# TensorE weights 128 columns wide in place of 125 in a fused Branchformer forward and backward kernel

## The chip, the cores and the metric

The kernel runs on one core of one Trainium2 chip, in one launch. The metric is device time in microseconds. Three runs of the kernel before gave 1264.24, 1264.71 and 1265.43 us, median 1264.71.

Names used below: PE is the matrix engine (TensorE), PEld its weight loads, DVE the vector engine, ACT the scalar engine, POOL the GpSimd engine, SP the engine that issues most DMAs. A product on PE has two operands: the *weights*, which are loaded into the array first by an instruction of their own, and the *moving* operand, whose columns are then streamed through. The number of weight columns is the number of output partitions; the number of moving columns is the free size of the output.

## The reference

One Branchformer layer, forward and gradient of all inputs, for x of shape 2 x 4000 x 144 in bf16. Cut to what matters:

```python
xa = _layernorm(x)
q, k, v = split(xa @ w_qkv)
p = softmax(q @ k.T * D ** -0.5)              # 4000 x 4000 for each of 2 batches
glob = (p @ v) @ w_att_out
u, g = split(gelu(_layernorm(x) @ w_mlp_in))
gc = sum(pad(_layernorm(g))[i:i+T] * dw_csgu[i] for i in range(5))
loc = (u * gc) @ w_mlp_out
m = concat(glob, loc); m = m + depthwise_conv5(m, dw_merge)
out = x + m @ w_merge
# returned: out and the vector-Jacobian products of grad_out for x and the seven weights
```

## The kernel before

The 4000 tokens of a batch are split into NB = 32 tiles of PB = 125 tokens. So nearly every weight operand that holds a tile of tokens is 125 columns wide. The four large buffers that hold such tiles already keep them 128 apart: P and dP scores in `Pb` and `SX`, their transposes PT and ST in `SX`. The three columns between are zeroed once by `pads` (line 953) for the score buffers, and the transposes on the DMA rings read and write all 128.

`phase_att` runs once per batch. It loops over t, the tile of queries. In each turn:

- `quad` (lines 1024 and 1030) makes score chunks of 125 x 500: for two chunks of scores (q of tile t) and two of dP (tile t-1) it issues four products with 128 rows of weights `QT` (line 1024, 500 moving columns), and then the four remaining products with 16 rows each (line 1030), whose weights stand in four different groups of 32 rows of the array and so can run side by side. I call the eight a quad.
- DVE takes the score chunks out of PSUM with a running minimum (line 1048), ACT takes the exponential (1056), ACT and DVE make P times dP (1066, 1069, 1071).
- The DMA rings transpose P into PT (1060) and P times dP into ST (1251).
- `Y_half` (1080) and `Z_half` (1126) run 32 products each over PT and ST with 145 and 144 moving columns. `X_group` (1171) runs products with the untransposed score buffers as weights and 144 moving columns, with a few more from `zt` and `dhT`; DVE adds them to the accumulator (1177).
- The units of the local branch (`local_units`) are dealt out over the turns. `t_unit` (595) transposes the gate and its gradient, with weights already 128 columns wide (`gdr`), into the tiles `gT` (line 502, five blocks of 125 columns). `gc_unit` (606, 607) and `dgn_unit` (621, 622) run the short convolution as ten products each, weights from `gT`, with 64 or 68 moving columns in eight of them and 32 or 34 in two. `dhT_unit` transposes `dhr` on the DMA ring.
- `jit_mm` (983, 984, 987), `z_unit` (526, 527) and `dug_unit` (558, 561) take weights straight from `R`, `xaT_m` and `goT`, where the tiles lie 125 apart.

After each batch, `Merge` computes the merged branch (1454, weights of 128 columns, is its largest part; 1551 and 1553 follow). The order of the instructions on every engine is written out by hand: `ORDER` lists it as differences of instruction numbers, and `Planner.plan` chains the instructions of an engine in that order. PE, DVE, ACT and POOL each run their list in order.

Of the kernel before, what the change touches and what calls it, by code (L numbers as in the profile page):

```python
# [15 lines left out]
D = 144  # L16
DR = 16
PB = 125
# [461 lines left out]
def local_units(k, W, b, S, A, es, DHT, ps_w):  # L480
# [21 lines left out]
    gT = [[pl.tile([128, 5, PB], BF, name="gT%d%d" % (a, i)) for i in range(2 + a)] for a in range(2)]  # L502
# [12 lines left out]
    for t_ in dhr:  # L515
        nc.gpsimd.memset(t_[:], 0.0)

# [72 lines left out]
    def t_unit(m):  # L590
        for a in range(2):
            pt = ps_w.tile([128, 5, 128], BF, tag="w")
            for j in range(5):
                x = 448 if j == 4 else 128 * j
                nc.tensor.transpose(pt[:, j, 0:PB], gv[:, a, place(m), x:x + 128], W.ident[0:PB, 0:PB])
            nc.scalar.copy(gT[a][m % (2 + a)][:], pt[:, :, 0:PB])
# [4 lines left out]
    def gc_unit(g):  # L601
        pc = ps_w.tile([PB, G2, D], F32, tag="w")
# [5 lines left out]
        nc.scalar.copy(gc[:], pc[:])  # L608
# [7 lines left out]
    def dgn_unit(g):  # L616
        pd = ps_w.tile([PB, G2, 9, 17], F32, tag="w")
        for n_, (m, x) in enumerate(wins(g)):
            t = gT[1][m % 3]
            for j in range(4):  # L620
                nc.tensor.matmul(pd[:, :, 2 * j:2 * j + 2, :].rearrange("p a b c -> p a (b c)"), t[:, j, :], W.eb[:, 8 * j + x:8 * j + x + 2, :], start=(n_ == 0 and j == 0), stop=(n_ == 1), skip_group_check=True)
            nc.tensor.matmul(pd[:, :, 8, :], t[:, 4, :], W.ebr[:, x:x + 2, :], start=False, stop=(n_ == 1), skip_group_check=True)
        rs, t = rsr[slot(g)], gd(g + 1, 0)
# [21 lines left out]
    def dhT_unit(g):  # L645
        dhT = sm.tile([128, 3 * G2, 128], BF, tag="dhT", bufs=3)
        nc.sync.dma_start_transpose(out=dhT[:], in_=dhr[g % 2][:].rearrange("p a b -> p (a b)"))
        for bi in range(G2):
            DHT[G2 * g + bi] = [dhT[:, 3 * bi + ct, 0:PB] for ct in range(3)]
# [71 lines left out]
for _s in """  # L721
PE 10 1 1 1 1 1 1 1 1 1 1 1 1 1 1 1 1 1 1 1 1 1 1 1 1 1 1 1 1 1 1 180 -179 182 -181 1 1 1 1 1 1 1 1 1 1 1 1 1 1 1 1 168 2 11 -180 1 1 1 1 1 1 1 1 1 1
# [33 lines left out]
DVE 9 127 -128 165 -14 31 1 5 -3 -1 5 -2 14 -15 18 -14 1 12 37 4 -51 -1 54 -52 1 47 -43 3 76 -81 44 -43 41 4 -21 -22 28 -23 19 6 -4 -19 78 -1 -76 1 1  # L756
# [47 lines left out]
Activation 148 1 -4 -1 2 78 -77 74 1 3 -74 80 4 -6 -79 77 13 1 22 89 5 -88 1 4 -32 30 83 -77 78 -6 8 -7 -49 6 1 4 4 37 -5 -20 6 4 -28 33 9 17 1 2 2 2  # L804
# [28 lines left out]
Pool 420 -260 24 251 -247 -2 -10 -39 50 -25 -23 293 -271 -21 294 2 -298 3 33 247 -244 27 -29 -33 95 -4 -48 -42 37 39 -37 100 -99 250 -157 4 -101 82  # L833
# [18 lines left out]
SP 0 172 -171 2 -1 151 -146 -3 1 149 -148 149 13 -16 19 -14 109 1 -101 3 -4 140 1 -136 -14 2 5 1 184 -16 1 -166 180 75 75 1 1 1 53 49 -47 -5 -45 5 13  # L852
# [17 lines left out]
class Planner:  # L870
# [24 lines left out]
    def plan(self, i0, i1):  # L895
# [23 lines left out]
        assert len(groups) == sum(len(v) for v in ORDER.values())  # L919
        order = ORDER  # L920
        for e in E:
            assert sorted(order[e]) == [x for x, g in enumerate(groups) if g["e"] == e]
        self.groups, self.order = groups, order
        for e in E:
            prev = None
            for g in order[e]:
# [6 lines left out]
def phase_att(k, W, b, S, A, M, head=None, late=None, extra=None):  # L933
# [6 lines left out]
    with ExitStack() as es:  # L940
# [24 lines left out]
        qbr = [qz[0:PB, QW * i:QW * i + 768].rearrange("p (a b) -> p a b", b=384)[:, :, 0:D] for i in range(3)]  # L965
        qrr = [qz[0:PB, QW * i + 128:QW * i + 384] for i in range(3)]
        znr = [qz[:, 3 * QW + 256 * i:3 * QW + 256 * (i + 1)] for i in range(2)]
# [33 lines left out]
        def jit_tr(i):  # L1001
            PL.tag("jt")
            qb = QB[i]
# [6 lines left out]
            for q, src in enumerate((qb[:, 0, 0:128], qrr[i % 3][:, 0:128], qrr[i % 3][:, 128:256], qb[:, 1, 0:128])):  # L1010
                nc.tensor.transpose(pt[:, q, 0:PB], src, W.ident[0:PB, 0:PB])
            qt = gw.tile([128, 4, 128], BF, tag="qt")
            nc.scalar.copy(qt[:, :, 0:PB], pt[:, :, 0:PB])
# [59 lines left out]
        def Y_half(i, h):  # L1073
            PL.tag("y%d" % h)
            if h == 0 and i not in YZ:
                yz = ps_yz.tile([PB, 2, 145], F32, tag="yz")
                YZ[i] = yz
# [969 lines left out]
```

## Time and profile before

| | |
|---|---|
| time, three runs | 1264.24 to 1265.43 us, median 1264.71 |
| profiled execution | span 1259.7 us from the first to the last instruction; no other time is listed for it, so the 5.0 us up to the median of the runs is taken as what lies around the span |
| granted TensorE clock, mean | 0.996 |
| PE busy | 1227.3 us, 15,890 products and as many weight loads |
| DVE, ACT, POOL busy | 1056.2, 740.4, 442.4 us |
| share of the chain that ended last | PE 74%, DVE 11%, DMA 9% |

How to read it: a row of instruction groups gives line, engine, operation, tile and shapes (partitions x columns; for PE the first pair is rows by columns of the weights), count, then busy time and mean duration. Durations of PE records overlap, since products are pipelined; the pace of products is seen in the chain view instead, whose rows are start, length and what ran, back to back. "issue" is time in which the engine waited for nothing that the profile shows.

### The profile page before, as it was taken

To read this page: it belongs to the slowest core of one execution; us is meant where nothing else is said; L and a number is where in the kernel's file an instruction comes from. 1 tells how busy PE (TensorE), PEld (TensorE's weight loads), DVE (VectorE), ACT (ScalarE), POOL (GpSimd) and SP (SyncE) were. 2 spreads that over 40 slices of the span, in tenths; PEclk is the share of its full clock that TensorE was granted. 3 is DMA by queue.
4 is the path that set the end of the run, shared out by engine and by line. 5 is a ranking of instruction groups with operands and counts; after the bars stand their busy time and mean duration, and the time that the engine had idled before them with its cause. 6 is when DMAs were issued, how large, how long until landed. Compare 5 with 4: busy or idle time off the path is not lost.

```text
span 1259.7 us, 38749 instructions
## 1 busy us (share of the span) xinstructions
PE 1227.3 (97%) x15890; PEld 1012.1 (80%) x15890; DVE 1056.2 (84%) x2862; ACT 740.4 (59%) x1183; POOL 442.4 (35%) x910
## 2 busy tenths in 40 slices
PE   9999999999999999999999999999999999999997
PEld 7777888878777878889887778788788888878996
DVE  8688989898988888879769898989888989887665
ACT  5866565556565655544746656565656565555273
POOL 8434333433333423213534423333334333232020
PEclk9999999999999999999999999999999999999998
DMA  3689988899989999985149989998898999999332
GB/s 106 129 146 151 158 157 157 156 151 154 168 146 157 158 151 159 158 193 159 65 101 157 161 158 164 155 160 146 145 173 151 155 157 162 172 167 188 96 103 69
DMA packets 638399, 186.52 MB, mean 148 GB/s; under 512 B 621025, under 2 KB 633164, under 8 KB 638214
## 3 DMA queue, kind: packets, MB, share of 16 engines
q1 hardware_dynamic: 616664, 176.66, 78.7%
q10 hardware_dynamic: 21348, 7.13, 3.0%
q8 instruction: 124, 2.03, 0.7%
q14 instruction: 55, 0.45, 0.1%
q0 software_dynamic: 208, 0.25, 0.1%
HBM read 20.82 MB, written 14.22 MB: 28 GB/s over the span
## 4 chain that ended last, share of the span: by engine, by line
PE 74%; DVE 11%; DMA 9%; ACT 2%; issue 2%; SPq 1%; POOL 1%; ACTq 0%; DVEq 0%
PE X L1171 17%; PE ps L1024 14%; PE yz L1126 9%; PE yz L1080 7%; PE ps L1030 6%; DMA SX<-SX 4%; PE Hps L1454 3%; PE po L1551 3%; DVE Pb L1048 3%; DMA SX<-Pb 2%; DVE acc L1177 1%; DMA qt<-qz 1%; PE pd L561 1%; PE pj L987 1%; PE pc L606 1%
## 5 line engine op out<-in xcount | busy, mean ns | idle before, releaser
L1048 DVE TENSOR_SCALAR_CACHE_REDUCE Pb<-ps 125x1000 bf16<-125x1000 f32 x256 | 306.2, 1197 | 75.8 <-PE ps L1030 71.5
L1056 ACT ACTIVATE Pb<-Pb,nm 125x1000 bf16<-125x1000 bf16 x256 | 277.4, 1127 | 120.5 <-DVE nm L1050 119.8
L1171 PE MATMUL X<-SX 125*125 125x144 bf16 x2048 | 300.1, 230 | 0.8 <-DVE acc L1175 0.7
L1171 PE MATMUL X<-SX,Pb 125*125 125x144 bf16 x2048 | 293.8, 226 | 0.0
L1069 ACT CAST SX<-ps 125x1000 bf16<-125x1000 f32 x189 | 187.9, 994 | 169.7 <-PE ps L1030 169.4
L1171 PEld LDWEIGHTS <-SX 125*125 125x125 bf16 x2048 | 259.8, 137 | 28.6 <-issue 28.0
L1024 PE MATMUL ps<-xaT_m,qt 128*125 128x500 bf16 x1024 | 262.2, 376 | 5.1 <-DVE Pb L1048 3.4
L1171 PEld LDWEIGHTS <-Pb 125*125 125x125 bf16 x2048 | 260.9, 137 | 1.4 <-issue 1.3
L1177 DVE TENSOR_TENSOR acc<-X,acc 125x432 f32<-125x432 f32 x372 | 200.9, 549 | 32.4 <-PE X L1171 31.2
L1126 PE MATMUL yz<-xa_aug,SX 125*125 125x144 bf16 x2048 | 153.0, 229 | 6.6 <-DMA SX<-SX 5.6
L1024 PEld LDWEIGHTS <-qt 128*125 128x125 bf16 x1024 | 122.1, 137 | 45.4 <-issue 5.0
L1126 PEld LDWEIGHTS <-SX 125*125 125x125 bf16 x2048 | 139.7, 138 | 14.0 <-DMA SX<-SX 7.8
L1080 PE MATMUL yz<-xa_aug,SX 125*125 125x145 bf16 x2048 | 145.9, 227 | 1.8 <-DMA SX<-Pb 1.8
L1080 PEld LDWEIGHTS <-SX 125*125 125x125 bf16 x2048 | 137.0, 137 | 3.2 <-DMA SX<-Pb 2.4
L1071 DVE TENSOR_TENSOR SX<-SX,Pb 125x1024 bf16<-125x1024 bf16 x189 | 130.8, 696 | 7.1 <-ACT SX L1069 4.8
L1030 PEld LDWEIGHTS <-qt 16*125 16x125 bf16 x1024 | 36.6, 128 | 99.7 <-issue 99.7
L1030 PE MATMUL ps<-XR,qt 16*125 16x500 bf16 x1016 | 112.1, 421 | 0.0
L1066 DVE TENSOR_TENSOR SX<-ps,Pb 125x1000 bf16<-125x1000 f32 x67 | 80.0, 1194 | 1.6 <-PE ps L1030 1.0
L635 POOL TENSOR_SCALAR l_w<-gdr,nc,c 125x144 f32<-125x144 bf16 x64 | 30.5, 480 | 97.1 <-DVE c L633 87.2
L531 POOL TENSOR_SCALAR l_a<-l_sq 125x576 bf16<-125x576 bf16 x32 | 23.1, 720 | 112.6 <-ACT l_sq L529 108.1
L1104 POOL TENSOR_SCALAR SX<-qz,rl 125x144 bf16<-125x144 bf16 x62 | 24.9, 402 | 96.9 <-DVE rl L1086 86.1
L999 POOL COPY qz<-qz 125x64 bf16<-125x64 bf16 (+1 forms) x124 | 33.4, 287 | 70.8 <-ACT qz L989 64.9
(474 smaller groups left out, 2179.4 us busy)
## 6 DMA issues: line engine op xcount, KB each, us to landing
go_h<-in_grad_out_dram SPq DMA_DIRECT2D x4, 567.0 KB
Yg<-ug_d SPq DMA_DIRECT2D x4, 567.0 KB
Yn_d<-yn ACTq DMA_DIRECT2D x64, 35.2 KB
Zn_d<-qz ACTq DMA_DIRECT2D x64, 35.2 KB
ug_d<-ugr ACTq DMA_DIRECT2D x32, 70.3 KB
SX<-in_x_dram SPq DMA_DIRECT2D x16, 140.6 KB
out_dram<-Pb SPq DMA_DIRECT2D x16, 140.6 KB
out_dram<-SX SPq DMA_DIRECT2D x16, 140.6 KB
```

What stands on the lines that cost most here:

```text
L1024: mm = nc.tensor.matmul(pp[r // 2][:, r % 2, 0:CH], QT[i][:, 3 * h, 0:PB], xaTm[:, c * CH:(c + 1) * CH], start=True, stop=False)
L1030: nc.tensor.matmul(pp[r // 2][:, r % 2, 0:CH], QT[i][rs, 1 + h, 0:PB], xr, start=False, stop=True)
L1048: nc.vector.tensor_scalar(pv(Pbuf, i % NPB, c2), src, -1.0, 3.0e38, op0=ALU.mult, op1=ALU.min, accum_out=NM[i][:, c2:c2 + 1])
L1056: nc.scalar.activation(v, v, ACT.Exp, bias=NM[i][:, 4:5], scale=-1.0)
L1066: nc.vector.tensor_tensor(pv(Sbuf, i % NDB, c2), src, pv(Pbuf, i % NPB, c2), op=ALU.mult)
L1069: nc.scalar.copy(pv(Sbuf, i % NDB, c2), src)
L1071: nc.vector.tensor_tensor(sc, sc, pchunk(i % NPB, c2), op=ALU.mult)
L1080: nc.tensor.matmul(Y, PT[0:PB, j, 0:PB], xaa[:, j, 0:D + 1], start=(j == 0), stop=(j == NB - 1))
L1126: nc.tensor.matmul(Z, ST[0:PB, j, 0:PB], xaa[:, j, 0:D], start=(j == 0), stop=(j == NB - 1))
L1171: nc.tensor.matmul(X[:, jj, :], l, r, start=(n_ == 0), stop=(n_ == len(ops) - 1))
L1177: nc.vector.tensor_tensor(av, X[:, 0:nj, :], av, op=ALU.add)
L1454: nc.tensor.matmul(H[a // 6][0:rows, a // 3 % 2, (a % 3) * D:(a % 3 + 1) * D], lhs, self.src[h][:, 2 + j, :], start=(j == 0 and a % 3 == 0 ...
```

## The change

Weights that hold a tile of tokens are taken 128 columns wide where the storage already allows it, and the PSUM tile under them has 128 partitions, of which the readers take the first 125. `gT` gets blocks of 128 columns, whose last three are zeroed once for each of its five tiles and each of the two batches (ten small memsets on POOL). The small transposes of q and z on PE take 128 rows. Left at 125 are the weights from `R`, `xaT_m` and `goT` (526, 527, 558, 561, 983, 984, 987), those of 1551 and 1553, and the last tile's transposes. No instruction but the memsets is added. The numbers in `ORDER` shift by five behind the memsets and by ten behind the second set; the sequence on every engine stays, with the memsets put behind those of `dhr` on POOL. The planner loses an attribute that nothing reads.

```diff
-    gT = [[pl.tile([128, 5, PB], BF, name="gT%d%d" % (a, i)) for i in range(2 + a)] for a in range(2)]
+    gT = [[pl.tile([128, 5, 128], BF, name="gT%d%d" % (a, i)) for i in range(2 + a)] for a in range(2)]
...
     for t_ in dhr:
         nc.gpsimd.memset(t_[:], 0.0)
+    for t_ in gT[0] + gT[1]:
+        nc.gpsimd.memset(t_[:, :, PB:128], 0.0)
...
-            nc.scalar.copy(gT[a][m % (2 + a)][:], pt[:, :, 0:PB])
+            nc.scalar.copy(gT[a][m % (2 + a)][:, :, 0:PB], pt[:, :, 0:PB])
...
-        pc = ps_w.tile([PB, G2, D], F32, tag="w")
+        pc = ps_w.tile([128, G2, D], F32, tag="w")
...
-        nc.scalar.copy(gc[:], pc[:])
+        nc.scalar.copy(gc[:], pc[0:PB])
...
-        pd = ps_w.tile([PB, G2, 9, 17], F32, tag="w")
+        pd = ps_w.tile([128, G2, 9, 17], F32, tag="w")
...
-            DHT[G2 * g + bi] = [dhT[:, 3 * bi + ct, 0:PB] for ct in range(3)]
+            DHT[G2 * g + bi] = [dhT[:, 3 * bi + ct, :] for ct in range(3)]
...
-            pp = [ps_sg.tile([PB, 2, 512], F32, tag="sg", name="ps") for _ in range(len(work) // 2)]
+            pp = [ps_sg.tile([128, 2, 512], F32, tag="sg", name="ps") for _ in range(len(work) // 2)]
...
-                mm = nc.tensor.matmul(pp[r // 2][:, r % 2, 0:CH], QT[i][:, 3 * h, 0:PB], xaTm[:, c * CH:(c + 1) * CH], start=True, stop=False)
+                mm = nc.tensor.matmul(pp[r // 2][:, r % 2, 0:CH], QT[i][:, 3 * h, :], xaTm[:, c * CH:(c + 1) * CH], start=True, stop=False)
...
-                    nc.tensor.matmul(pp[r // 2][:, r % 2, 0:CH], QT[i][rs, 1 + h, 0:PB], xr, start=False, stop=True)
-            return [p[:, :, 0:CH].rearrange("p h (a b) -> p h a b", b=PB) for p in pp]
+                    nc.tensor.matmul(pp[r // 2][:, r % 2, 0:CH], QT[i][rs, 1 + h, :], xr, start=False, stop=True)
+            return [p[0:PB, :, 0:CH].rearrange("p h (a b) -> p h a b", b=PB) for p in pp]
...
-                nc.tensor.matmul(Y, PT[0:PB, j, 0:PB], xaa[:, j, 0:D + 1], start=(j == 0), stop=(j == NB - 1))
+                nc.tensor.matmul(Y, PT[0:PB, j, :], xaa[:, j, 0:D + 1], start=(j == 0), stop=(j == NB - 1))
...
-                nc.tensor.matmul(Z, ST[0:PB, j, 0:PB], xaa[:, j, 0:D], start=(j == 0), stop=(j == NB - 1))
+                nc.tensor.matmul(Z, ST[0:PB, j, :], xaa[:, j, 0:D], start=(j == 0), stop=(j == NB - 1))
...
-                    ops.append((Sbuf[0:PB, i % NDB, j * 128:j * 128 + PB], QBs[:, i % NPB, 0, :]))
-                    ops.append((Pbuf[0:PB, i % NPB, j * 128:j * 128 + PB], QBs[:, i % NPB, 1, :]))
+                    ops.append((Sbuf[0:PB, i % NDB, j * 128:j * 128 + 128], QBs[:, i % NPB, 0, :]))
+                    ops.append((Pbuf[0:PB, i % NPB, j * 128:j * 128 + 128], QBs[:, i % NPB, 1, :]))
...
-                    ops += [(zt[:, q, 0:PB], W.M1T[:, q, :]) for q in range(2)]
+                    ops += [(zt[:, q, :], W.M1T[:, q, :]) for q in range(2)]
```

More of the change, by code (lines that the diff above doesn't have):

```diff
@@ L622, in dgn_unit @@
             nc.tensor.matmul(pd[:, :, 8, :], t[:, 4, :], W.ebr[:, x:x + 2, :], start=False, stop=(n_ == 1), skip_group_check=True)
+        pd = pd[0:PB]
         rs, t = rsr[slot(g)], gd(g + 1, 0)
@@ L721 @@
 for _s in """
-PE 10 1 1 1 1 1 1 1 1 1 1 1 1 1 1 1 1 1 1 1 1 1 1 1 1 1 1 1 1 1 1 180 -179 182 -181 1 1 1 1 1 1 1 1 1 1 1 1 1 1 1 1 168 2 11 -180 1 1 1 1 1 1 1 1 1 1
[3 rows of a table removed]
+PE 10 1 1 1 1 1 1 1 1 1 1 1 1 1 1 1 1 1 1 1 1 1 1 1 1 1 1 1 1 1 1 185 -184 187 -186 1 1 1 1 1 1 1 1 1 1 1 1 1 1 1 1 173 2 11 -185 1 1 1 1 1 1 1 1 1 1
[3 rows of a table added]
  -6 34 -32 39 -25 32 -28 2 48 -46 3 5 14 6 14 2 18 -44 46 -14 1 17 10 18 -7 -2 10 9 -5 2 20 -13 2 9 6 1 24 -6 2 10 5 17 -7 -2 10 8 -4 8 2 2 11 -9 3 10
@@ L755 @@
  187 3 -18 -159 6 172 -169 3 163 -160 3 11 1 13 2 1 13
-DVE 9 127 -128 165 -14 31 1 5 -3 -1 5 -2 14 -15 18 -14 1 12 37 4 -51 -1 54 -52 1 47 -43 3 76 -81 44 -43 41 4 -21 -22 28 -23 19 6 -4 -19 78 -1 -76 1 1
+DVE 9 127 -128 165 -14 36 1 5 -3 -1 5 -2 14 -15 18 -14 1 12 37 4 -51 -1 54 -52 1 47 -43 3 76 -81 44 -43 41 4 -21 -22 28 -23 19 6 -4 -19 78 -1 -76 1 1
  69 1 -23 25 1 -38 -39 75 -16 6 -24 22 4 13 -36 17 -18 2 1 35 -39 48 -7 -1 16 -14 20 -19 17 -2 6 46 -35 3 4 -2 6 -2 28 -22 34 14 1 53 14 -22 31 -29
@@ L803 @@
  -22 19 -166 1 1 1 1 1 1 1 1 3 -2 176 -169 1 1 1 1 1 1 1 1 3 180 -19 -163 179 -145 1 1 1 1 1 1 1 1 3 -2 7 1 1 1 1 1 1 1 1 3 -2
-Activation 148 1 -4 -1 2 78 -77 74 1 3 -74 80 4 -6 -79 77 13 1 22 89 5 -88 1 4 -32 30 83 -77 78 -6 8 -7 -49 6 1 4 4 37 -5 -20 6 4 -28 33 9 17 1 2 2 2
+Activation 148 1 -4 -1 2 83 -82 79 1 3 -79 85 4 -6 -84 82 13 1 22 89 5 -88 1 4 -32 30 83 -77 78 -6 8 -7 -49 6 1 4 4 37 -5 -20 6 4 -28 33 9 17 1 2 2 2
  1 21 -2 -15 2 2 12 -8 -2 4 4 7 2 4 4 4 7 -5 6 176 -174 173 -170 142 -122 -19 20 34 -30 -2 3 2 1 108 -99 20 -22 62 -64 28 10 2 56 2 -68 13 2 13 9 39
@@ L832 @@
  -232 3 216 -213 28 179 -204 41 6 1 2 3 153 -150 28 -25 41
-Pool 420 -260 24 251 -247 -2 -10 -39 50 -25 -23 293 -271 -21 294 2 -298 3 33 247 -244 27 -29 -33 95 -4 -48 -42 37 39 -37 100 -99 250 -157 4 -101 82
[18 rows of a table removed]
-SP 0 172 -171 2 -1 151 -146 -3 1 149 -148 149 13 -16 19 -14 109 1 -101 3 -4 140 1 -136 -14 2 5 1 184 -16 1 -166 180 75 75 1 1 1 53 49 -47 -5 -45 5 13
+Pool 425 -265 24 256 -252 -2 -10 -39 50 -25 -23 298 -276 -21 299 2 -303 3 33 252 -249 32 -34 -33 100 -4 -53 -42 37 44 -42 105 -104 255 -157 4 -106 87
[18 rows of a table added]
+SP 0 172 -171 2 -1 151 -146 -3 1 149 -148 149 13 -16 19 -14 114 1 -106 3 -4 145 1 -141 -14 2 5 1 189 -16 1 -171 185 75 75 1 1 1 53 49 -47 -5 -45 5 13
  70 14 -73 15 -2 106 36 -29 20 14 45 29 -22 13 71 -57 50 29 -9 68 -54 -228 275 35 -9 14 52 -7 32 5 -14 -382 378 62 42 5 -40 26 54 8 -1 31 -10 66 -51
@@ L893, in count, with grouped @@
         return n
-    def plan(self, i0, i1):
+    def grouped(self, i0, i1):
         E = {"PE": "PE", "DVE": "DVE", "Activation": "ACT", "Pool": "POOL", "SP": "SP"}
@@ L918, in plan @@
                 groups.append(dict(e=e, ins=[ins], x=x + i0, t=None, sg=False, rem=False))
[L919 to L924, printed above, removed]
+        return groups
+    def plan(self, i0, i1):
+        groups = self.grouped(i0, i1)
+        for e, order in ORDER.items():
+            assert sorted(order) == [x for x, g in enumerate(groups) if g["e"] == e]
             prev = None
-            for g in order[e]:
+            for g in order:
                 for i in groups[g]["ins"]:
@@ L965, in phase_att @@
         qbr = [qz[0:PB, QW * i:QW * i + 768].rearrange("p (a b) -> p a b", b=384)[:, :, 0:D] for i in range(3)]
+        qbf = [qz[:, QW * i:QW * i + 768].rearrange("p (a b) -> p a b", b=384)[:, :, 0:128] for i in range(3)]
         qrr = [qz[0:PB, QW * i + 128:QW * i + 384] for i in range(3)]
+        qrf = [qz[:, QW * i + 128:QW * i + 384] for i in range(3)]
         znr = [qz[:, 3 * QW + 256 * i:3 * QW + 256 * (i + 1)] for i in range(2)]
@@ L1002, in jit_tr @@
             PL.tag("jt")
-            qb = QB[i]
             if i > (0 if head is None else 2):
@@ L1009, in jit_tr @@
             pt = ps_w.tile([128, 4, 128], BF, tag="w")
-            for q, src in enumerate((qb[:, 0, 0:128], qrr[i % 3][:, 0:128], qrr[i % 3][:, 128:256], qb[:, 1, 0:128])):
-                nc.tensor.transpose(pt[:, q, 0:PB], src, W.ident[0:PB, 0:PB])
+            for q, src in enumerate((qbf[i % 3][:, 0], qrf[i % 3][:, 0:128], qrf[i % 3][:, 128:256], qbf[i % 3][:, 1])):
+                nc.tensor.transpose(pt[:, q, :], src, W.ident[:])
             qt = gw.tile([128, 4, 128], BF, tag="qt")
-            nc.scalar.copy(qt[:, :, 0:PB], pt[:, :, 0:PB])
+            nc.scalar.copy(qt[:], pt[:])
             QT[i] = qt
@@ L1075, in Y_half @@
             if h == 0 and i not in YZ:
-                yz = ps_yz.tile([PB, 2, 145], F32, tag="yz")
+                yz = ps_yz.tile([128, 2, 145], F32, tag="yz")
                 YZ[i] = yz
@@ L1079, in Y_half @@
             for j in range(16 * h, 16 * h + 16):
-                nc.tensor.matmul(Y, PT[0:PB, j, 0:PB], xaa[:, j, 0:D + 1], start=(j == 0), stop=(j == NB - 1))
+                nc.tensor.matmul(Y, PT[0:PB, j, :], xaa[:, j, 0:D + 1], start=(j == 0), stop=(j == NB - 1))
             if h == 0:
                 return
+            Y = Y[0:PB]
             qb = QB.pop(i)
@@ L1121, in Z_half @@
             if h == 0 and i + 1 not in YZ:
-                yz = ps_yz.tile([PB, 2, 145], F32, tag="yz")
+                yz = ps_yz.tile([128, 2, 145], F32, tag="yz")
                 YZ[i + 1] = yz
@@ L1129, in Z_half @@
             zn = znr[i % 2]
-            nc.vector.scalar_tensor_tensor(zn[0:PB, 0:D], Z, RL.pop(i)[:], TY.pop(i)[:], op0=ALU.mult, op1=ALU.add)
+            nc.vector.scalar_tensor_tensor(zn[0:PB, 0:D], Z[0:PB], RL.pop(i)[:], TY.pop(i)[:], op0=ALU.mult, op1=ALU.add)
             nc.scalar.dma_start(S.Zn_d[:, i, :], zn[0:PB, 0:D])
@@ L1143, in zt_tr @@
             for q in range(2):
-                nc.tensor.transpose(pt[:, q, 0:PB], zn[0:PB, q * 128:(q + 1) * 128], W.ident[0:PB, 0:PB])
-            nc.scalar.copy(zt[:, :, 0:PB], pt[:, 0:2, 0:PB])
+                nc.tensor.transpose(pt[:, q, :], zn[:, q * 128:(q + 1) * 128], W.ident[:])
+            nc.scalar.copy(zt[:], pt[:, 0:2, :])
         def X_groups(t):
@@ L1158, in X_group @@
             nj = len(blocks)
-            X = ps_w.tile([PB, 3, D], F32, tag="w")
+            X = ps_w.tile([128, 3, D], F32, tag="w")
             for jj, j in enumerate(blocks):
@@ L1174, in X_group @@
                 seen.update(blocks)
-                nc.vector.tensor_copy(av, X[:, 0:nj, :])
+                nc.vector.tensor_copy(av, X[0:PB, 0:nj, :])
             else:
-                nc.vector.tensor_tensor(av, X[:, 0:nj, :], av, op=ALU.add)
+                nc.vector.tensor_tensor(av, X[0:PB, 0:nj, :], av, op=ALU.add)
         seen = set()
@@ L1202, in jit_q @@
             pt = ps_w.tile([128, 4, 128], BF, tag="w")
-            for q, src in enumerate((QB[i][:, 0, 0:128], qrr[i % 3][:, 0:128])):
-                nc.tensor.transpose(pt[:, q, 0:PB], src, W.ident[0:PB, 0:PB])
-            nc.scalar.copy(QT[i][:, 0:2, 0:PB], pt[:, 0:2, 0:PB])
+            for q, src in enumerate((qbf[i % 3][:, 0], qrf[i % 3][:, 0:128])):
+                nc.tensor.transpose(pt[:, q, :], src, W.ident[:])
+            nc.scalar.copy(QT[i][:, 0:2, :], pt[:, 0:2, :])
         def jit_b(i):
@@ L1217, in jit_b @@
             pt = ps_w.tile([128, 4, 128], BF, tag="w")
-            for q, src in enumerate((qrr[i % 3][:, 128:256], QB[i][:, 1, 0:128])):
-                nc.tensor.transpose(pt[:, q, 0:PB], src, W.ident[0:PB, 0:PB])
-            nc.scalar.copy(QT[i][:, 2:4, 0:PB], pt[:, 0:2, 0:PB])
+            for q, src in enumerate((qrf[i % 3][:, 128:256], qbf[i % 3][:, 1])):
+                nc.tensor.transpose(pt[:, q, :], src, W.ident[:])
+            nc.scalar.copy(QT[i][:, 2:4, :], pt[:, 0:2, :])
         if head is None:
```

54 rows, old and new, of the table ORDER are left out of this document.

## The prediction

> **What bounds the kernel now.** I read the page's totals and the chain that ended last first, then the weight loads by shape, then the chain row by row, and last the waits.
>
> ```profile
> span 1259.7 us, 38749 instructions
> PE 1227.3 (97%) x15890; PEld 1012.1 (80%) x15890; DVE 1056.2 (84%) x2862; ACT 740.4 (59%) x1183; POOL 442.4 (35%) x910
> PE 74%; DVE 11%; DMA 9%; ACT 2%; issue 2%; SPq 1%; POOL 1%; ACTq 0%; DVEq 0%
> PE X L1171 17%; PE ps L1024 14%; PE yz L1126 9%; PE yz L1080 7%; PE ps L1030 6%; DMA SX<-SX 4%; PE Hps L1454 3%; PE po L1551 3%; DVE Pb L1048 3%; DMA SX<-Pb 2%; DVE acc L1177 1%; DMA qt<-qz 1%; PE pd L561 1%; PE pj L987 1%; PE pc L606 1%
> ```
>
> PE is busy almost without a break and holds three quarters of the chain. So a shorter PE stream shortens the kernel, as long as no other engine is close behind. The loads by shape (behind the first bar: busy us and mean ns) show what one weight load takes:
>
> ```profile
> L1080 PEld LDWEIGHTS <-SX 125*125 125x125 bf16 x2048 | 137.0, 137 | 3.2 <-DMA SX<-Pb 2.4 <-issue 0.7
> L1126 PEld LDWEIGHTS <-SX 125*125 125x125 bf16 x2048 | 139.7, 138 | 14.0 <-DMA SX<-SX 7.8 <-issue 6.0
> L1171 PEld LDWEIGHTS <-Pb 125*125 125x125 bf16 x2048 | 260.9, 137 | 1.4 <-issue 1.3
> L1171 PEld LDWEIGHTS <-SX 125*125 125x125 bf16 x2048 | 259.8, 137 | 28.6 <-issue 28.0 <-DVE acc L1177 0.2 <-ACT l_sq L529 0.2
> L595 PEld LDWEIGHTS <-gdr 125*128 125x128 bf16 x180 | 11.0, 98 | 3.8 <-issue 3.1 <-POOL qz L999 0.2 <-POOL A_dwc L654 0.2
> L1030 PEld LDWEIGHTS <-qt 16*125 16x125 bf16 x1024 | 36.6, 128 | 99.7 <-issue 99.7
> L195 PEld LDWEIGHTS <-Pb 16*128 16x128 bf16 x4 | 0.4, 92 | 0.6 <-issue 0.5
> L606 PEld LDWEIGHTS <-gT 128*125 128x125 bf16 x256 | 19.4, 138 | 2.4 <-issue 2.4
> L621 PEld LDWEIGHTS <-gT 128*125 128x125 bf16 x256 | 19.3, 138 | 1.6 <-issue 1.6
> ```
>
> 125 columns take 137 ns and 128 columns 98, both with 125 rows: three more columns are loaded 39 ns faster. With 16 rows it is 128 against 92, 36 ns. So the change has an effect on every load it touches; the question is which of these loads PE waits for. **That is read from the chain**, where products follow each other (start, length, what):
>
> ```profile
> 283.15 0.85 PE ps L1024 x4
> ...
> 285.00 1.01 PE yz L1126 x16
> ...
> 294.46 0.36 PE ps L1030 x4
> 294.82 0.66 PE pt L595 x10
> ...
> 300.60 0.36 PE ps L1030 x4
> 300.96 1.16 PE yz L1126 x16
> ...
> 302.62 0.20 PE pc L606 x4
> 302.82 0.04 PE pc L607
> 302.86 0.25 PE pc L606 x4
> 303.11 0.04 PE pc L607
> ```
>
> ```profile
> 234.98 0.55 PE pt L595 x10
> ```
>
> ```profile
> 574.88 1.13 PE Hps L1454 x18
> ```
>
> Three things are to be seen. First, 16 products of 144 moving columns with 125-column weights take 1.01 us, 63 ns each, and line 1454, whose weights are 128 wide, needs 1.13 / 18 = 63 ns too. There the moving columns set the pace and the load is hidden. Second, right behind a quad the same 16 take 1.16, 0.15 more; ten transposes with 128-column weights take 0.66 behind a quad and 0.55 elsewhere, 0.11 more. A switch from 16-row groups to the whole array costs about 0.11 anyway, and a slow first load adds 0.04 that nothing hides. Third, the convolution's ten products take 0.20 + 0.04 + 0.25 + 0.04 = 0.53 us though they move only 64 or 32 columns. Ten transposes that move 125 columns need 0.55: the loads set the pace here.
>
> **The change, part by part.** *Products of lines 1080, 1126 and 1171* (2048, 2048 and 4096, together 8192; a few hundred more of 1171 from other tiles) and of line 1024: nothing, by 63 against 63 ns. The cover is the moving of 144 or 500 columns; without it each load costs 39 ns less, which is the next two parts.
>
> *The quads' own loads.* The waits tell how many there are:
>
> ```profile
> PEld L1030 <- issue: 99.7, 264, 0.7
> PEld L1171 <- issue: 29.2, 128, 0.8
> PEld L1126 <- issue: 6.0, 24, 0.8
> PEld L606 <- issue: 2.4, 11, 0.2
> PEld L621 <- issue: 1.6, 7, 0.2
> PEld L1126 <- DMA SX<-SX: 7.8, 12, 1.6
> PE yz L1126 <- DMA SX<-SX: 5.6, 7, 1.4
> ```
>
> Before each of 264 groups the weight loader stands still for 99.7 / 264 = 0.38 us, until line 1024 has streamed out; only then are the four 16-row loads made, side by side, and nothing covers them. 264 x 36 ns (128 less 92) = 9.5 us. The bounds are 0, if loads into four row groups keep the slow form, which no row shows with 128 columns, and 264 x 39 = 10.3. I take 9.5, since the 92 ns row has the same 16 rows.
>
> *The first load behind a quad.* The next four rows count those whose weights become 128 wide: 128 + 24 + 11 + 7 = 170. 170 x 39 = 6.6 us; the chain's 0.15 less 0.11 gives 6.8. I take 6.6, with 0 below if the switch itself grows.
>
> *The convolution.* There are 256 / 8 = 32 units in line 606 and as many in 621, 64 in all. If loads no longer set the pace, the moving columns do. Pace against columns: ten transposes of 125 columns in 0.55 (55 ns), 144 columns in 63 ns, and 500 columns in 0.85 / 4 = 212. That is 0.42 ns a column and about 3 ns, so 64 columns need 30 ns; for the two short products I take 20 ns, the 58 of before less 39. Ten: 8 x 30 + 2 x 20 = 0.28 us in place of 0.53, 0.25 saved, 64 x 0.25 = 16.0 us. The bounds: no row shows a pace below 55 ns with 128-column weights in a run of products; if 45 were the floor, 64 x (0.53 - 0.45) = 5 us; the upper end is 16. I take 16, since the short products are nearer to the straight line of three rows than to a floor that no row shows.
>
> *The memsets.* Ten of 15 columns on POOL, as long as this one, five per batch:
>
> ```profile
> L953 POOL MEMSET SX<- 125x15 bf16 x1 | 0.1, 110 | 0.0
> ```
>
> ```profile
> 48.84 0.67 POOL L531 TENSOR_SCALAR l_a<-l_sq 125x576 bf16<-125x576 bf16 x1 [11.39 <-ACT l_sq L529]
> ```
>
> 5 x 0.11 = 0.55 us each time. In the first batch ten small operations of line 305 are queued behind and then line 531 with 11.39 us of idle time before it, so it is covered. In the second batch line 531 stands right behind with no such rest, and DVE and ACT wait for it in turn; between 0 and 0.55 us. I take 0, with PE's own queue as the cover. No wait is added on any other engine, and the DMA list is the same. The small transposes of q and z (24 of them, three more columns of 0.42 ns) and their copies are below 0.1 us.
>
> PE's stream thus gets shorter by 9.5 + 6.6 + 16.0 = 32.1 us. **How much of it reaches the end.** Only what lies on the chain counts. Of 264 x 0.36 = 95 us of line 1030, the chain by line, in the page's row above, holds 6% of 1259.7 = 76 us, a share of 0.80. 32.1 x 0.80 = 25.7. The other engines must then keep a faster pace:
>
> ```profile
> 120.00:160.00 40.00, 39.85 (x490) 31.81 (x489) 37.34 (x102) 24.98 (x37) 14.32 (x29) 1.00 1.01 160
> ```
>
> These 40 us hold 39.85 us of PE, 31.81 of its loads and 37.34 of DVE; the last three figures are the granted clock, the share of the DMA engines and GB/s. PE loses about 1.0 us of work in such a stretch (32.1 / 1259.7 x 40). DVE has 2.7 us to spare, so it can follow, but some waits will grow: products of 1126 for the transposes on the rings, of 1024 for DVE's line 1048. I take a tenth off: 23 us, a judgement. The profiled span would be 1236.7 and the time, with the 5.0 us around the span that make up the median, 1241.7; I say 1241, and 1233 to 1247 for this case alone.
>
> The Trainium skill, "TensorE: Matmul & The Clock Gate", has two rules for this, which speak against each other. Its section "LDWEIGHTS (loading the stationary operand)" lets a load grow with its columns, 125 / 1.2 = 104 ns and 128 / 1.2 = 107; by that alone the change is no gain. Its section "Weight-path perf modes" says that a fast weight load is used when there are exactly 128 weight columns and the type is not fp32; the rows of 98 against 137 ns agree with this one, and the sum goes by those rows.
>
> **The rivals.** (a) *The other engines keep the time.* The DMA share of 1.01 in the row above and DVE at 37.34 of 40 speak for it; against it, PE is hardly ever idle there. In the chain there are stretches where a transposition holds the end, such as
>
> ```profile
> 260.95 8.19 DMA SX<-SX
> ```
>
> If these spread so that two thirds of 32.1 turn into new waits, 11 us are left: 1254.
>
> (b) *The 16-row loads stay slow*, as they go to four row groups at once: (6.6 + 16.0) x 0.80 less a tenth = 16 us, 1248. The row of 92 ns shows one load at a time.
>
> (c) *The change doesn't do what it says*: loads of 128 columns are not faster in these places, and grow by 3 / 125 of their 137 ns, 3 ns. Then 434 open loads (264 + 170) and 640 in the convolution cost 1074 x 3 ns = 3 us at the most: 1265 to 1268. The two loads of 98 ns from different tiles speak against it. The skill's rule on columns, named above, is this rival.
>
> (d) *Slower: a fast load disturbs the moving stream.* In line 1171 the weights and the moving operand come from the same buffer `SX`, in line 1454 from two. If the pace there went from 63 to 68 ns, and in 1080 and 1126 with it, 8192 x 5 ns x 0.80 = 33 us would be lost against 23 gained: 1275. It decides from 23 / (8192 x 0.80) = 3.5 ns a product. Against it stand the 63 ns of line 1454 and the 55 of line 595.
>
> **How the numbers follow.** The forecast gets 0.60, (a) 0.20, (b) 0.08, (c) 0.04, (d) 0.08. The time is that of the forecast. Its upper end is that of (a) and a little more, 1256; the lower is all of the 32.1 us with 2 to spare for loads behind other stops, 1230. That leaves out (c), (d) and a part of (a), and little below, less than 2 in 10. Faster by over 0.2% (2.5 us, about what these runs can tell from no change) are the forecast, (a) and (b), 0.88; (c) is nearly all within it, 0.04; slower is (d), 0.08.
>
> **What the profile after would show.** Right: loads of lines 1080, 1126, 1171, 1024, 606 and 621 at 98 ns and of 1030 at 92; four products of 1030 at 0.32 us on the chain; 16 of 1126 behind a quad at 1.12 and elsewhere still 1.01; a convolution unit at 0.28; DVE and the DMA rings busy as long as before in a shorter span. Wrong: loads still at 137 ns (c); 1030 at 128 (b); a pace of 66 or more in 1126 or 1171 (d); or waits of line 1126 for `SX<-SX` that grow by over 10 us from the 7.8 + 5.6 of before (a).

## The result, and the profile after

The changed kernel takes 1249.71 us (median of 4 runs, 1247.25 to 1254.23) against 1265.07 for the kernel before on the same chip. The medians are 15.4 us apart. The ratio on record, which is not the quotient of the medians (the two differ by up to 0.13% in the runs here), is 0.9889, 95% interval 0.986 to 0.9918: about 14 us faster, between 10 and 18. A second measurement, told below, gave 0.9882 (0.9862 to 0.9902). The profiled execution has a span of 1246.7 us, 13.0 less than that of before. The forecast was 1241 with a range of 1230 to 1256.

Line numbers are two to five higher now: 1084, 1131 and 1176 are the products Y, Z and X (before: 1080, 1126, 1171), 1028 and 1034 the quads (1024, 1030), 608 with 609 and 623 with 624 the convolution (606, 607, 621, 622).

The loads by shape of the kernel after (count, then busy us and mean ns):

```profile
L1176 PEld LDWEIGHTS <-Pb 125*128 125x128 bf16 x2048 | 200.2, 98 | 3.7 <-issue 3.1
L1131 PEld LDWEIGHTS <-SX 125*128 125x128 bf16 x2048 | 132.8, 98 | 20.7 <-DMA SX<-SX 13.8 <-issue 6.2
L1084 PEld LDWEIGHTS <-SX 125*128 125x128 bf16 x2048 | 132.6, 98 | 6.7 <-DMA SX<-Pb 5.6 <-issue 0.4
L1034 PEld LDWEIGHTS <-qt 16*128 16x128 bf16 x1024 | 26.6, 91 | 111.3 <-issue 111.3
L623 PEld LDWEIGHTS <-gT 128*128 128x128 bf16 x256 | 11.7, 98 | 1.5 <-issue 1.5
L608 PEld LDWEIGHTS <-gT 128*128 128x128 bf16 x256 | 11.2, 97 | 2.6 <-issue 2.4
```

All six are fast: 97 or 98 ns in place of 137 or 138, and 91 in place of 128 for the 16-row loads in four row groups. The chain of the kernel after, row by row (start, length, what):

```profile
205.32 1.01 PE yz L1131 x16
...
210.41 0.32 PE ps L1034 x4
...
211.59 0.12 PE pc L608 x4
211.71 0.01 PE pc L609
211.72 0.13 PE pc L608 x4
211.85 0.01 PE pc L609
```

```profile
294.05 0.66 PE pt L597 x10
```

```profile
949.38 1.12 PE yz L1131 x16
```

The products of X, first behind a quad and then elsewhere, in the kernel before and in the changed one:

```profile
291.41 0.90 PE X L1171 x12
286.02 0.75 PE X L1171 x12
```

```profile
210.73 0.86 PE X L1176 x12
295.73 0.75 PE X L1176 x12
```

Four products of a quad take 0.32 us on the chain (0.36 before); 16 products of Z take 1.01 as before, and 1.12 behind a quad (1.16); 12 products of X take 0.75 as before, and 0.86 behind a quad (0.90); the transposes behind a quad, whose weights were 128 wide already, take 0.66 as before; a convolution unit takes 0.12 + 0.01 + 0.13 + 0.01 = 0.27 us in place of 0.53. So PE's stream became shorter where the prediction said, and by about what it said: 264 x 0.04 + 170 x 0.04 + 64 x 0.26 = 34 us by these rows, against 32.1 forecast. Less than half of that is left at the end. The totals and the chain after:

```profile
span 1246.7 us, 38759 instructions
PE 1202.6 (96%) x15890; PEld 947.8 (76%) x15890; DVE 1053.6 (85%) x2862; ACT 739.3 (59%) x1183; POOL 444.9 (36%) x920
PE 62%; DVE 15%; DMA 14%; ACT 6%; issue 2%; SPq 1%; POOL 1%; ACTq 0%; DVEq 0%; POOLq 0%
PE X L1176 14%; PE ps L1028 11%; PE yz L1131 8%; DMA SX<-SX 6%; PE yz L1084 5%; PE ps L1034 5%; DMA SX<-Pb 4%; DVE Pb L1052 4%; PE Hps L1459 3%; PE po L1556 3%; ACT Pb L1060 2%; DVE acc L1182 2%; DVE SX L1075 2%; DMA qt<-qz 1%; PE warm L154 1%
```

PE's busy time fell by 24.7 us and the span by only 13.0: PE stands idle for 1246.7 - 1202.6 = 44.1 us, 11.7 more than before (1259.7 - 1227.3 = 32.4). Why the busy time fell by less than the 34 us of the rows wasn't found out; in the pair with both cuts, below, it fell by 35.2. PE's share of the chain fell from 74% to 62%; the DMA rings gained 5 points, DVE and ACT 4 each. The waits name most of the new idle time (total us, times, longest). First three rows of the kernel before, then the kernel after:

```profile
PE yz L1080 <- DMA SX<-Pb: 1.8, 3, 0.7
PE ps L1024 <- DVE Pb L1048: 3.4, 6, 1.6
PE ps L1024 <- DMA qt<-qz: 1.5, 4, 0.5
```

```profile
PEld L1131 <- DMA SX<-SX: 13.8, 18, 2.7
PE yz L1131 <- DMA SX<-SX: 9.5, 11, 2.6
PEld L1084 <- DMA SX<-Pb: 5.6, 7, 1.1
PE yz L1084 <- DMA SX<-Pb: 4.1, 7, 0.9
PE ps L1028 <- DVE Pb L1052: 5.2, 11, 1.7
PE ps L1028 <- DMA qt<-qz: 3.1, 5, 0.9
```

Z's waits for the transposed P times dP, the first two rows of the kernel after, were 7.8 and 5.6 us. Of the rows of PE itself (those of PEld are its loader's), the transposes took 9.5 + 4.1 + 3.1 = 16.7 us in place of 5.6 + 1.8 + 1.5 = 8.9, and the quads' wait for DVE to empty their PSUM tiles 5.2 in place of 3.4: together 9.6 of the 11.7 us of new idle time.

### The profile page after: what moved, and what is told of

It reads as the page before. It is cut to its first block, busy times and chain, and to the rows that moved or that the text cites. A ratio compares the mean times of both kernels' runs of the same rounds, so it can differ in the third digit from the quotient of the medians.

```text
span 1246.7 us, 38759 instructions
## 1 busy us (share of the span) xinstructions
PE 1202.6 (96%) x15890; PEld 947.8 (76%) x15890; DVE 1053.6 (85%) x2862; ACT 739.3 (59%) x1183; POOL 444.9 (36%) x920
## 4 chain that ended last, share of the span: by engine, by line
PE 62%; DVE 15%; DMA 14%; ACT 6%; issue 2%; SPq 1%; POOL 1%; ACTq 0%; DVEq 0%; POOLq 0%
PE X L1176 14%; PE ps L1028 11%; PE yz L1131 8%; DMA SX<-SX 6%; PE yz L1084 5%; PE ps L1034 5%; DMA SX<-Pb 4%; DVE Pb L1052 4%; PE Hps L1459 3%; PE po L1556 3%; ACT Pb L1060 2%; DVE acc L1182 2%; DVE SX L1075 2%; DMA qt<-qz 1%; PE warm L154 1%
## 5 line engine op out<-in xcount | busy, mean ns | idle before, releaser
L1176 PE MATMUL X<-SX 125*128 125x144 bf16 x2048 | 294.5, 227 | 2.0 <-DVE acc L1180 0.7
L1176 PE MATMUL X<-SX,Pb 125*128 125x144 bf16 x2048 | 293.8, 226 | 0.0
L1028 PE MATMUL ps<-xaT_m,qt 128*128 128x500 bf16 x1024 | 262.2, 376 | 8.7 <-DVE Pb L1052 5.2
L1176 PEld LDWEIGHTS <-SX 125*128 125x128 bf16 x2048 | 197.3, 97 | 28.9 <-issue 27.7
L1176 PEld LDWEIGHTS <-Pb 125*128 125x128 bf16 x2048 | 200.2, 98 | 3.7 <-issue 3.1
L1131 PE MATMUL yz<-xa_aug,SX 125*128 125x144 bf16 x2048 | 151.6, 229 | 11.6 <-DMA SX<-SX 9.5
L1084 PE MATMUL yz<-xa_aug,SX 125*128 125x145 bf16 x2048 | 145.7, 227 | 4.1 <-DMA SX<-Pb 4.1
L1131 PEld LDWEIGHTS <-SX 125*128 125x128 bf16 x2048 | 132.8, 98 | 20.7 <-DMA SX<-SX 13.8
L1028 PEld LDWEIGHTS <-qt 128*128 128x128 bf16 x1024 | 91.0, 98 | 71.1 <-issue 8.4
L1084 PEld LDWEIGHTS <-SX 125*128 125x128 bf16 x2048 | 132.6, 98 | 6.7 <-DMA SX<-Pb 5.6
L1034 PEld LDWEIGHTS <-qt 16*128 16x128 bf16 x1024 | 26.6, 91 | 111.3 <-issue 111.3
L1034 PE MATMUL ps<-XR,qt 16*128 16x500 bf16 x1016 | 102.1, 382 | 0.0
## 6 DMA issues: line engine op xcount, KB each, us to landing
Yn_d<-yn ACTq DMA_DIRECT2D x64, 35.2 KB
Zn_d<-qz ACTq DMA_DIRECT2D x64, 35.2 KB
```

The costliest lines, as they stand in the source:

```text
L1028: mm = nc.tensor.matmul(pp[r // 2][:, r % 2, 0:CH], QT[i][:, 3 * h, :], xaTm[:, c * CH:(c + 1) * CH], start=True, stop=False)
L1034: nc.tensor.matmul(pp[r // 2][:, r % 2, 0:CH], QT[i][rs, 1 + h, :], xr, start=False, stop=True)
L1084: nc.tensor.matmul(Y, PT[0:PB, j, :], xaa[:, j, 0:D + 1], start=(j == 0), stop=(j == NB - 1))
L1131: nc.tensor.matmul(Z, ST[0:PB, j, :], xaa[:, j, 0:D], start=(j == 0), stop=(j == NB - 1))
L1176: nc.tensor.matmul(X[:, jj, :], l, r, start=(n_ == 0), stop=(n_ == len(ops) - 1))
```

## The experiments

### The three parts alone

Two theories were set against each other. By F, a fixed share of what PE saves reaches the end, so that each part alone gains in proportion. By L, the other engines allow about 14 us and no more, so that a part alone comes through nearly whole. The three kernels are the kernel before with some of the hunks of the change each.

`e1_conv`: the convolution's weights and the memsets.

```diff
-    gT = [[pl.tile([128, 5, PB], BF, name="gT%d%d" % (a, i)) for i in range(2 + a)] for a in range(2)]
+    gT = [[pl.tile([128, 5, 128], BF, name="gT%d%d" % (a, i)) for i in range(2 + a)] for a in range(2)]
...
+    for t_ in gT[0] + gT[1]:
+        nc.gpsimd.memset(t_[:, :, PB:128], 0.0)
```

> Only the convolution's weights gT are 128 wide (with the ten memsets); all else as before. Both theories: loads of gT at 98 ns, a unit of ten products at 0.28 us in place of 0.53, PE stream shorter by 16 us. Theory F (a fixed share: of each microsecond that PE saves, about 0.44 reach the end, as 14 of 32 did together, because the chain is on PE only part of the time): 16 x 0.44 = 7 us faster, ratio 0.9944. Theory L (a limit: the other engines and the rings allow about 14 us and no more, whatever PE saves): the first 14 us come through nearly whole, 13 to 14 us faster, ratio 0.989.

Measured: 1255.15 us against 1263.02, ratio 0.9947 (0.9929 to 0.9965). By the ratio that is 6.7 us faster, by the medians 7.9; the three parts are compared here by the ratios.

`e2_quads`: the weights of the quads, lines 1024 and 1030.

```diff
-                mm = nc.tensor.matmul(pp[r // 2][:, r % 2, 0:CH], QT[i][:, 3 * h, 0:PB], xaTm[:, c * CH:(c + 1) * CH], start=True, stop=False)
+                mm = nc.tensor.matmul(pp[r // 2][:, r % 2, 0:CH], QT[i][:, 3 * h, :], xaTm[:, c * CH:(c + 1) * CH], start=True, stop=False)
...
-                    nc.tensor.matmul(pp[r // 2][:, r % 2, 0:CH], QT[i][rs, 1 + h, 0:PB], xr, start=False, stop=True)
+                    nc.tensor.matmul(pp[r // 2][:, r % 2, 0:CH], QT[i][rs, 1 + h, :], xr, start=False, stop=True)
```

> Only the quads' weights QT are 128 wide (lines 1024 and 1030 and the small transposes that make QT); all else as before. Both: loads of 1030 at 91 ns, PE stream shorter by 264 x 38 ns = 10 us. Theory F: 10 x 0.44 = 4.4 us faster, ratio 0.9965. Theory L: 9 to 10 us faster, ratio 0.9925.

Measured: 1255.22 us, ratio 0.9944 (0.9931 to 0.9957), 7.1 us faster.

`e3_xyz`: the weights of X, Y and Z, here cut to Z.

```diff
-                nc.tensor.matmul(Z, ST[0:PB, j, 0:PB], xaa[:, j, 0:D], start=(j == 0), stop=(j == NB - 1))
+                nc.tensor.matmul(Z, ST[0:PB, j, :], xaa[:, j, 0:D], start=(j == 0), stop=(j == NB - 1))
```

> Only the weights of Y, Z and X (PT, ST, the score buffers, zt, dhT) are 128 wide, 8192 products and more; all else as before. Loads at 98 ns in place of 137. Pace inside a run unchanged at 63 ns, so only the first load behind a quad is saved, about 156 x 39 ns = 6 us of PE's stream. Theory F: 2.7 us faster, ratio 0.998. Theory L: 5 to 6 us faster, ratio 0.995. If the hidden loads had cost something after all, more than 6.

Measured: 1258.07 us, ratio 0.9963 (0.9947 to 0.9979), 4.7 us faster.

Neither theory holds as it was put. The convolution returned 6.7 of 16 us, as F said; the quads returned 7.1 of 10, midway between F's 4.4 and L's 9 to 10; X, Y and Z returned 4.7 of 6, nearer to L, with F's 2.7 at the edge of the interval. The sum of the parts is 0.53 + 0.56 + 0.37 = 1.46%, 18 us, and together they gave 1.11% and 1.18% in the two measurements. That the whole is less than its parts points to a competition for the same slack, but the intervals overlap, so it isn't shown. That e3 gains no more than its first loads behind a quad allow (128 + 24 = 152 of the 170; the other 18 are the convolution's) fits with the thousands of other loads of lines 1080, 1126 and 1171 being hidden. The gain alone can't show it, since other engines may hold back a larger saving; the rows above do: 16 products of Z take 1.01 us and 12 of X 0.75, with slow loads and with fast ones.

### Which cover PE bumped into

The next four kernels take work away from one suspect, in the kernel before and in the changed one; they leave out parts of the results and serve only to measure. The difference within a pair is what the change is worth when that suspect is lighter. Cut on the rings (from the second tile on, the second half of Y's products then has no new transpose to wait for):

```diff
-            nc.sync.dma_start_transpose(out=PT[:], in_=Pbuf[:, i % NPB, :])
+            n = NB // 2 if i else NB
+            nc.sync.dma_start_transpose(out=PT[:, 0:n, :], in_=Pbuf[:, i % NPB, 0:n * 128])
...
-                    a, w = h * NB // 2, NB // 2
+                    a, w = h * NB // 2, NB // 2 if t == 1 else NB // 4
```

> The kernel before, with the transposes of P (line 1060) and of P times dP (line 1251) on the DMA rings cut to half their columns from the second tile on; Y and Z run all 32 products, half of them over old data. It leaves out half of that transposition, nothing else. This is the base of the pair with e6_after_rings. The chain of before holds 46.3 + 28.5 us of these transposes, so both theories expect it faster than before, by 10 to 60 us.

> The changed kernel with the same halving. What counts is the difference to e5_before_rings. Theory R (the rings' transposes swallowed the missing gain of about 18 us): with them halved, 25 us or more of the 32 come through, so e6 is 25 to 32 us faster than e5. Theory V (the vector engine swallowed it): the difference stays near the 14 us of the whole kernels, 10 to 18. Theory O (many small waits of every kind, set by the fixed order): in between, 16 to 24, here and in the other pair.

Cut on DVE:

```diff
-                sc = Sbuf[0:PB, i % NDB, c2 * 1024:(c2 + 1) * 1024]
-                nc.vector.tensor_tensor(sc, sc, pchunk(i % NPB, c2), op=ALU.mult)
+                sc = Sbuf[0:PB, i % NDB, c2 * 1024:c2 * 1024 + 512]
+                nc.vector.tensor_tensor(sc, sc, pchunk(i % NPB, c2)[:, 0:512], op=ALU.mult)
...
-                nc.vector.tensor_tensor(av, X[:, 0:nj, :], av, op=ALU.add)
+                nc.vector.tensor_tensor(av[:, :, 0:72], X[:, 0:nj, 0:72], av[:, :, 0:72], op=ALU.add)
```

> The kernel before, with two vector operations on half their columns: the product of P and dP in line 1071 (512 of 1024) and the addition to the accumulator in line 1177 (72 of 144). It leaves out half of these two results, nothing else; DVE has about 150 us less to do of its 1056. Base of the pair with e8_after_dve. Expected: faster than before by 5 to 40 us.

> The changed kernel with the same two operations halved. Difference to e7_before_dve: theory V 25 to 32 us, theory R 10 to 18, theory O 16 to 24.

And both cuts at once, which was chosen after the results of these four:

> The kernel before with both cuts: the transposes of P and of P times dP on the rings at half their columns, and lines 1071 and 1177 on DVE at half theirs. It leaves out those halves of the results. Base of the pair with e10_after_both. If rings and DVE are the covers that PE bumps into, it is faster than each cut alone (1248.5 and 1258.3 us): 1240 to 1246.

> The changed kernel with both cuts. Difference to e9_before_both. Theory O (the missing gain went into waits for the rings and for DVE both, each of which came back in part when it alone was cut: 23 and 20 us): with both cut, 27 to 32 us, nearly the 32 that PE saves. Theory P (something else, such as the clock, the fixed order or PE's own stream, keeps a part whatever the other engines do): the difference stays at the larger of the two, 20 to 25 us.

Measured, medians in us:

| cut | kernel before | changed kernel | difference |
|---|---|---|---|
| none | 1263.5 | 1248.2 | 15.3 |
| rings (e5, e6) | 1248.5 | 1224.8 | 23.7 |
| DVE (e7, e8) | 1258.3 | 1238.3 | 20.0 |
| both (e9, e10) | 1244.3 | 1212.1 | 32.2 |

(The row without a cut is from the runs beside e9 to e12.) The ratios to before are 0.9893 and 0.9712 for the rings, 0.9969 and 0.9814 for DVE, 0.9861 and 0.9604 for both, each within 0.003 or less. Relative to its own base the change is worth 1.2% without a cut, 1.8% with lighter rings, 1.6% with a lighter DVE and 2.6% with both; the difference of two such figures is uncertain by about 0.4 of a point. So the step from none to both is far outside the noise, and the steps from none to the rings and from the rings to both are outside it; the step from none to DVE alone, 0.4, is at its edge. The pairs with one cut lie too close together to say which of the two weighs more.

With both covers lighter, the change brings 32.2 us, and 32.1 was what it takes off PE's stream. The pair is uncertain by about 4 us, so that the two agree to a tenth is luck. Theory O holds (16 to 24 with one cut, 27 to 32 with both), R and V each explain a part, and P falls. The clock is no rival here: in both kernels the runs with a lower granted clock are longer, and at the same clock the spans are as far apart, 1246.5 and 1213.9 us at 0.993, 1243.0 and 1211.1 at 0.996. The totals and the chain of e9, then of e10:

```profile
span 1243.0 us, 38680 instructions
PE 1222.8 (98%) x15890; PEld 1010.9 (81%) x15890; DVE 946.4 (76%) x2862; ACT 739.8 (60%) x1183; POOL 434.1 (35%) x910
PE 93%; DVE 3%; ACT 2%; DMA 1%; issue 1%; POOL 0%; SPq 0%; DVEq 0%; ACTq 0%; POOLq 0%
```

```profile
span 1208.7 us, 38690 instructions
PE 1187.6 (98%) x15890; PEld 943.3 (78%) x15890; DVE 942.7 (78%) x2862; ACT 737.8 (61%) x1183; POOL 435.5 (36%) x920
PE 91%; DVE 4%; ACT 3%; DMA 1%; issue 1%; POOL 0%; SPq 0%; ACTq 0%; DVEq 0%; POOLq 0%
```

The chain is nearly all PE's in both, and stays so when PE gets faster. With one cut the chain of the changed kernel moves to the cover that was left. First e6, with lighter rings, then e8, with a lighter DVE:

```profile
PE 71%; DVE 19%; ACT 4%; issue 2%; DMA 2%; POOL 1%; ACTq 0%; SPq 0%; DVEq 0%; POOLq 0%
```

```profile
PE 74%; DMA 15%; DVE 4%; ACT 4%; issue 1%; SPq 1%; POOL 1%; ACTq 0%; DVEq 0%; POOLq 0%
```

DVE has 19% of the chain in one and DMA 15% in the other. DVE's cut was smaller than expected, 110 us of its busy time in place of 150, and the kernel before gained only 3.8 us by it, where 5 to 40 had been expected. The other two bases came out as expected, and the pairs as theory O said, with 32.2 just above its 32.

### Wider still

`e4_wide` is the changed kernel with the weights from `R`, `xaT_m` and `goT` 128 wide too; in the rows that count the three more columns are those of the next tile.

```diff
-            ti = slice(i * PB, (i + 1) * PB)
-            pj = ps_w.tile([PB, 2 * D], F32, tag="w")
-            nc.tensor.matmul(pj[:], R[:, ti], W.RW[:, 0:2 * D], start=True, stop=False)
...
+            n = 128 if i < NB - 1 else PB
+            ti = slice(i * PB, i * PB + n)
+            pj = ps_w.tile([128, 2 * D], F32, tag="w")
+            nc.tensor.matmul(pj[0:n], R[:, ti], W.RW[:, 0:2 * D], start=True, stop=False)
```

> The changed kernel, with the weights from R, xaT_m and goT (lines 526, 527, 558, 561, 983, 984, 987) taken 128 wide too, the three columns more being those of the next tile; the last tile of a batch stays at 125. 48 of these first loads stand right behind a quad, so PE saves 48 x 39 ns = 2 us more. Theory F: 1 us faster than the changed kernel, ratio to before 0.988. Theory L: the same as the changed kernel, 0.989.

It gave 1246.07 us, ratio 0.9869 (0.9854 to 0.9883), which could have been better than the changed kernel. So both ran again beside each other.

> The changed kernel once more, beside e12 on the same chip, to narrow its interval: the sum of the three parts alone was 0.53 + 0.56 + 0.37 = 1.46%, together 1.11% with an interval of 0.82 to 1.40. Theory L (the parts compete for the same slack): again 0.8 to 1.2% faster than before. Parts that simply add: 1.4 to 1.5%.

> The kernel of e4_wide once more beside the changed one. PE saves 48 x 39 ns = 2 us more than in the changed kernel; at the share that came through, 1 us or 0.1%, so 0.9989 of the changed kernel or the same within the interval. If e4's 0.9869 was more than chance, 0.998.

The changed kernel: 1248.16 us, 0.9882 (0.9862 to 0.9902). The wider one: 1250.14 us, 0.9902 (0.9879 to 0.9926). The first lead did not come back; the two can't be told apart, and there is no version here that is shown to beat the changed kernel. Three of the wider kernel's six runs had a granted clock of 0.991 or 0.992 and took 1251.5 to 1254.0 us; the other three, at 0.996 or 0.997, took 1246.4 to 1248.8. Its PE was busy for 1195.2 and 1195.6 us in the two profiles, against 1202.6 and 1201.1 for the changed kernel, and the time did not follow: again it isn't PE alone that sets the end.

## Why the prediction came out as it did

The time, 1249.7 us, lies in the range of 1230 to 1256 because its upper end was taken from rival (a). It is outside the 1233 to 1247 that the prediction gave for its own case. What PE saves was right, how much of it reaches the end was not.

*The loads* came out as the rows of before said: 39 ns less, and 37 for the 16-row loads, also in four row groups at once. Rivals (b) and (c) fall. The rule of the Trainium skill ("TensorE: Matmul & The Clock Gate", section "Weight-path perf modes") that a fast load comes with exactly 128 columns agrees with all six groups of loads shown.

*The hidden loads* of X, Y and Z were worth nothing, as forecast, and the pace stayed at 63 ns in Z (1.01 / 16) and in X (0.75 / 12), so rival (d) falls as well, though X takes both operands from `SX`.

*The quads' own loads, the first load behind a quad, and the convolution* were right in place and size: 0.36 to 0.32, 1.16 to 1.12 and 0.53 to 0.27 us, where 0.32, 1.12 and 0.28 had been put. The two short products of a convolution unit had 0.04 us each on the chain before, where the prediction took 58 ns, and 0.01 after, where it put 20 ns; the other eight took 0.25 us in place of 0.24. The sum of 32.1 us agrees with the pair with both cuts, 32.2, within the 4 us of that pair.

*The memsets* took 116 ns each (110 had been put). What they cost at the end was not measured: e1 has them, but together with the faster convolution.

*How much of it reaches the end* is the term that was mis-sized. The prediction took the share of line 1030 on the chain, 0.80, and a tenth off that for new waits, together 23 us. It measured 14, less than half of 32.1. Two things went wrong there. A chain tells what held the end at each moment and not by how much: a stretch can belong to PE with another engine a little behind. And DVE's idle time of 2.7 us in 40 was read as room enough for 1.0 us, though what counts is not DVE's total but how late each of its results may come in an order that is written out by hand. Rival (a), that the other engines keep the time, named the mechanism and both engines, with 1254; the truth lies between it and the forecast. Its sign was that Z's waits for `SX<-SX` grow by over 10 us from 7.8 + 5.6. They grew by 9.9 in the profile after, and by 12.5 in the profile of the second measurement (15.4 + 10.5), so the sign came at its threshold. But it looked at these waits alone, and the pairs show that DVE holds a part beside the rings.

*Span and time.* The 5.0 us around the span are not what lies around it: in all 53 runs of this kernel and of the changed one for which both are on record, the time is 1.7 to 1.8 us above the span. The profiled execution of before was thus a short one, of about 1261.5 us. The forecast is not changed by this, since adding the 5.0 comes to the same as taking the 23 us from the median.

What stays open is how the missing part divides. The waits put 7.8 of PE's 9.6 us of new waiting down to the transposes, but the transposes of P times dP can start only when DVE and ACT have made it, so some of this may be DVE's. Why the convolution alone returned 0.42 of its saving and the quads 0.7 was not found out.

## What to carry to other kernels

Look at the mean duration of weight loads by shape before counting columns: here three columns of padding made a load 39 ns shorter, but this is worth time only where nothing is moved over it, that is at switches between row-grouped and whole-array products, and in products with fewer moving columns than the load takes. Where the bounding engine gets faster in a kernel with a fixed order, the rest of the engines may take back a good part: here more than half, though the bounding engine was busy for 97% of the span. The share of the chain is not the share of the gain. To find out who takes it, lighten each suspect in both kernels and compare the pairs.

## What was not expected of the hardware

In the profiled execution of the changed kernel the clock was granted at half for 6.8 us between 44 and 52 us, in the head of the kernel, and for some 3.4 us more from 74 to 80; the profiled execution of the second measurement had none there. The stretch from 40 to 80 us, first run and then the second (the third figure from the end is the clock):

```profile
40.00:80.00 40.00, 37.92 (x362) 24.30 (x359) 28.29 (x64) 27.41 (x55) 16.24 (x30) 0.87 0.67 133
```

```profile
40.00:80.00 40.00, 37.14 (x406) 24.70 (x405) 31.96 (x72) 30.43 (x60) 16.59 (x32) 1.00 0.80 151
```

The first started 362 products in that stretch and the second 406, and yet the spans were 1246.7 and 1246.9 us. The second lost its clock elsewhere: it was granted 0.93 from 1050 to 1100 us and 0.97 from 1100 to 1150, where the first had 1.00. That is 5.0 us of full clock lost there against 5.2 in the head of the first, and the means over the span are 0.994 and 0.993. So the place where the clock drops changes from one execution of the same kernel to the next, and one stretch of a single profile should not be compared without its clock.
